# Attention and two gated layers on one core: long fillers on TensorE ahead of the first chunk, another price for the weights' low bits, and a new table of due times

## The chip, the cores and the metric

The kernel runs on one core of a Trainium2 chip. Its engines are TensorE (PE; its weight loads are listed apart as PEld), VectorE (DVE), ScalarE (ACT), GpSimd (POOL) and SyncE (SP), which here only issues DMAs. The metric is the device time of one execution in microseconds. Three runs of the kernel before gave 923.89, 925.21 and 926.55, so the median is 925.21.

## The reference

Attention over q, k, v of shape 4 x 8 x 576 x 64, once over means of four neighbouring rows and once in a band of width 7, then two layers over 2304 tokens of width 512 (weights arrive as 64-bit floats):

```python
out_d = sm_attn(q_d, k_d, v_d)                 # softmax attention over means of 4 rows
out_up = np.repeat(out_d, factor, axis=2)
mask = np.abs(pos[:, None] - pos[None, :]) < factor
scores = scale * np.matmul(q, k.transpose(0, 1, 3, 2))
scores = np.where(mask, scores, -1000000000.0)  # softmax, then @ v: out_local
attn_out = out_up + out_local
x = np.ascontiguousarray(attn_out.transpose(0, 2, 1, 3)).reshape(B * S, H * D)
h = x @ w_in                                   # 512 x 2048
g = np.where(h > 0.0, h, alpha * (np.exp(np.minimum(h, 0.0)) - 1.0))
x = g @ w_out                                  # 2048 x 512
silu = g2 * (1.0 / (1.0 + np.exp(-g2)))        # g2 = x @ w_gate, 512 x 1536
return silu * (x @ w_val) @ w_out2             # 1536 x 512
```

## The kernel before, in words

Nearly every large product is done as three products of two halves (high and low part of each 32-bit operand): `products` issues hi*hi, hi*lo and lo*hi at L1060, L1061 and L1062. The second matrix of the first chunk is the exception, one 32-bit product (L1094).

**Stages.** Tokens of the first layer go in chunks of 288 (three units of 96). The head, ahead of the first chunk, is the attention of the first batch. q and k rows are turned on TensorE (`add_first_batch`, L779) and copied out by ACT and DVE. Four pairs of heads of pooled attention follow (`add_pooled`: scores L857, weights turned L900, values L916). So do six units of local attention (`add_local`: scores L674, mask L692, maxima L697, values L745). Three units make the first chunk's `x`: the sum of both attentions (L1037), its high part (L369 or L371), its low part (L1048). Meanwhile 32 weight tiles arrive, and each is made from its 64-bit words by three operations. These are the low bits (`rest`, L532 on DVE or L534 on ACT), the size (L528 on ACT, into a PSUM bank) and the joining of both (L538 on DVE). An "in" weight is then split: high part L373 on POOL or L369 on ACT, low part L573 on POOL.

**The first chunk** (`add_whole`) takes sixteen rounds. A round is 12 products from `x` into a bank `h`, then an ELU in three steps (ACT L1099, ACT L1100, DVE L1101), then four products L1094 of an earlier round. `h` may lie in two banks only, 6 or 7 (L1081). The ELU's last step gives `h` free.

**What sets the order.** A list scheduler of the kernel's own (`Work`) writes each engine's static order at build time. Every piece of work has a due time and a cost per engine. The table of constants at the top shifts due times, and `start` takes the earliest due piece whose buffers are free. `fetched` lets TensorE's instructions arrive in blocks of 256 words, with `FETCHES` as the time of a block. Where TensorE has nothing ready in the head, `fill` issues a filler product: a short one of 64 columns up to `SHORT` words, a long one of 512 columns later. `warm_up` issues 72 short products at the start. SP issues all loads in one order as well.

**Banks in the head.** Units' scores take banks by this rule, in which `begun` is set when the first product of the first chunk is issued:

```python
def att_bank(late=False):
    return banks.new(lambda: [4, 5] if begun else [6, 0, 1, 2, 3])
```

A bank that holds scores is free when DVE has masked them (L692). The first chunk's sums lie in banks 0 to 3.

## Time and profile before

| | us |
|---|---|
| median of three runs | 925.21 |
| the profiled execution | 921.95 |
| its span, first to last instruction | 920.0 |
| TensorE busy in the span | 905.5 |
| DVE, ACT, POOL busy | 558.6, 520.0, 531.5 |

The profiled execution is 1.95 us longer than its span, and 3.26 us shorter than the median of the runs. TensorE is busy for 98% of the span, so what counts is where it is not busy, and when it does work that is no part of the result (warm-up and fillers). The mean granted clock of TensorE is 0.998 of full speed.

### The profile page before, as it was taken

How to read it: one execution, taken by the hardware profiler on the slowest of the kernel's cores; microseconds unless marked ns; L12 is line 12 of the kernel's file. 1: busy time of each engine (PE TensorE's matmuls, PEld its weight loads, DVE VectorE, ACT ScalarE, POOL GpSimd, SP SyncE). 2: the span in 40 equal slices, each digit the busy share in tenths (PEclk: the TensorE clock that was granted, in tenths of full speed). 3: DMA queues.
4: the chain of work that ended last, by engine and by line, in shares of the span. 5: the costliest groups of instructions: out<-in, count | busy, mean ns of one | idle time of the engine just before them, and what ended most of it. 6: DMA issues, size and time to landing. Idle time of an engine off the chain costs nothing.

```text
span 920.0 us, 20707 instructions
## 1 busy us (share of the span) xinstructions
PE 905.5 (98%) x7937; PEld 818.5 (89%) x7937; DVE 558.6 (61%) x958; ACT 520.0 (57%) x1140; POOL 531.5 (58%) x607
## 2 busy tenths in 40 slices
PE   8799999999999999999999999999999999999998
PEld 6588898989999999999999888888888888999998
DVE  6889877765576349443358475343333258997672
ACT  6888665454556456767555566566545335444441
POOL 6686965655666357698892226989999910000000
PEclk9999999999999999999999999999999999999999
DMA  8999545678645763656497615464624299755231
GB/s 184 325 269 249 102 137 129 131 274 240 119 134 132 222 184 130 226 184 212 167 341 281 238 69 183 160 240 160 240 82 183 81 297 324 260 172 161 92 127 47
DMA packets 193251, 172.17 MB, mean 187 GB/s; under 512 B 96064, under 2 KB 164160, under 8 KB 193152
## 3 DMA queue, kind: packets, MB, share of 16 engines
q1 hardware_dynamic: 193008, 170.58, 59.3%
q8 instruction: 63, 1.03, 0.5%
q14 instruction: 36, 0.29, 0.1%
q10 hardware_dynamic: 144, 0.26, 0.1%
HBM read 111.62 MB, written 59.18 MB: 186 GB/s over the span
## 4 chain that ended last, share of the span: by engine, by line
PE 93%; DMA 3%; DVE 1%; ACT 1%; issue 1%; SPq 1%; ACTq 0%
PE bank L1060 29%; PE bank L1061 28%; PE bank L1062 28%; PE bank L1094 3%; PE bank L674 2%; PE bank L745 2%; DMA w<-in_v_dram 1%; DMA w<-in_k_dram 1%; PE bank L965 1%; PE bank L959 1%; PE bank L1012 1%; PE warm L1753 1%; SPq L770 0%; DVE f L1037 0%; SPq L619 0%
## 5 line engine op out<-in xcount | busy, mean ns | idle before, releaser
L1062 PE MATMUL bank<-xs,wu 128*128 128x512 f32 x336 | 133.2, 396 | 0.0
L1061 PE MATMUL bank<-xs,wu 128*128 128x512 f32 x336 | 133.2, 396 | 0.0
L1060 PE MATMUL bank<-xs,wu 128*128 128x512 f32 x336 | 133.1, 396 | 0.0
L1060 PE MATMUL bank<-os,ys 128*128 128x256 f32 x378 | 107.1, 283 | 0.5 <-DVE o L1273 0.5
L1061 PE MATMUL bank<-os,ys 128*128 128x256 f32 x378 | 107.0, 283 | 0.0
L1062 PE MATMUL bank<-os,ys 128*128 128x256 f32 x378 | 106.9, 283 | 0.0
L1273 DVE TENSOR_TENSOR blk<-bank,blk 128x512 f32<-128x512 f32 x72 | 49.8, 691 | 93.6 <-PE bank L1062 86.6
L1060 PE MATMUL bank<-x,w 128*128 128x288 f32 x320 | 100.3, 314 | 1.9 <-DVE e L1138 1.4
L1060 PE MATMUL bank<-g,w 128*128 128x288 f32 (+1 forms) x320 | 101.0, 316 | 0.0
L1061 PE MATMUL bank<-g,w 128*128 128x288 f32 (+1 forms) x320 | 98.5, 308 | 0.0
L1062 PE MATMUL bank<-g,w 128*128 128x288 f32 (+1 forms) x320 | 98.4, 307 | 0.0
L1062 PE MATMUL bank<-x,w 128*128 128x288 f32 x320 | 94.5, 295 | 0.2 <-issue 0.2
L1061 PE MATMUL bank<-x,w 128*128 128x288 f32 x320 | 94.7, 296 | 0.0
L1270 ACT COPY blk<-bank 128x512 f32<-128x512 f32 x72 | 42.2, 586 | 86.4 <-PE bank L1062 82.5
L1145 POOL TENSOR_TENSOR g<-e,g 128x288 fp32r<-128x288 f32 x64 | 55.4, 867 | 52.2 <-ACT g L369 36.0
L1062 PEld LDWEIGHTS bank<-xs,wu 128*128 128x128 f32 x336 | 63.3, 188 | 15.4
L1061 PEld LDWEIGHTS bank<-xs,wu 128*128 128x128 f32 x336 | 63.3, 188 | 14.2
L1060 PEld LDWEIGHTS bank<-xs,wu 128*128 128x128 f32 x336 | 63.3, 188 | 14.2
L1060 PEld LDWEIGHTS bank<-os,ys 128*128 128x128 f32 x378 | 72.5, 192 | 0.9 <-DVE o L1273 0.7
L1061 PEld LDWEIGHTS bank<-os,ys 128*128 128x128 f32 x378 | 72.5, 192 | 0.2
L1062 PEld LDWEIGHTS bank<-os,ys 128*128 128x128 f32 x378 | 72.5, 192 | 0.0
L1241 POOL TENSOR_TENSOR wu<-s,wu 128x256 fp32r<-128x256 f32 x77 | 60.1, 807 | 12.3 <-ACT wu L1244 12.0
(221 smaller groups left out, 2503.4 us busy)
## 6 DMA issues: line engine op xcount, KB each, us to landing
yr<-yd SPq DMA_DIRECT2D x27, 512.0 KB
yd<-blk SPq DMA_DIRECT2D x24, 512.0 KB
os<-od SPq DMA_DIRECT2D x42, 256.0 KB
w<-in_moe_w_in_dram SPq DMA_DIRECT2D x16, 512.0 KB
w<-in_moe_w_out_dram SPq DMA_DIRECT2D x16, 512.0 KB
wp<-w SPq DMA_DIRECT2D x16, 512.0 KB
wu<-wp SPq DMA_DIRECT2D x16, 512.0 KB
u<-wd SPq DMA_DIRECT2D x32, 256.0 KB
```

The source lines that it names most:

```text
L674: nc.tensor.matmul(sc[j].t[s * QB:(s + 1) * QB, (u * NP + p) * QB:(u * NP + p + 1) * QB], parts["qT"][p].t[j * D:(j + 1) * D, a:a + QB], p ...
L745: nc.tensor.matmul(pvs[r].t[j * D:(j + 1) * D, k * 2 * SB:(k + 1) * 2 * SB], tvs[u].t[rows, (2 * p + j) * D:(2 * p + j + 1) * D], bd.t[row ...
L959: nc.tensor.matmul(sc[0].t[j * D:(j + 1) * D, 2 * G:3 * G], vs0.t[:, w, j], prT0.t[:, j, w], start=(w == 0), stop=(w == 1))
L965: nc.tensor.matmul(sc[j].t[:HALF, u * G:(u + 1) * G], t[:, 0, p, u * HALF:(u + 1) * HALF], t[:, 1, p], start=True, stop=True)
L1060: nc.tensor.matmul(ps, sh, mh, start=first, stop=False, skip_group_check=more)
L1061: nc.tensor.matmul(ps, sh, ml, start=False, stop=False, skip_group_check=more)
L1062: nc.tensor.matmul(ps, sl, mh, start=False, stop=last, skip_group_check=more)
L1094: nc.tensor.matmul(acc[0][i].t[:, :T1], wo.t[:, i * P:(i + 1) * P].bitcast(F32), ge(), start=f == 0, stop=f == NF1 - 1)
L1145: add("pool", 0.86, due - URGENT, lambda e=e, g=g: nc.gpsimd.tensor_tensor(out=g.t[:, 1], in0=e.t, in1=g.t[:, 0], op=ALU.subtract), reads= ...
L1241: return task(engines, n, due, lambda engine=engines[0]: two(engine).tensor_tensor(out=out(), in0=in0(), in1=in1(), op=op), reads, writes, ...
L1270: return add("act", ps_copy, when(m) - 20, lambda: nc.scalar.copy(d(i), ps.t[:, :w]), reads=[ps], writes=of(i))
L1273: return add("dve", ps_sum, when(m) - 20, lambda: nc.vector.tensor_tensor(out=d(i), in0=ps.t[:, :w], in1=d(i), op=ALU.add), reads=[ps], wr ...
```

## The change

Four things change in the code. The warm-up is ten products of 512 columns instead of 72 of 64. `fill` has its long form alone. The planner's price for the low bits on DVE doubles (0.5 to 1.0) and a block of instructions costs it 7.4 instead of 6.0; the price of the pooled weights on ACT rises from 1.28 to 1.66. And nearly all due times of the table move (two of some sixty stand here).

```diff
-    SECOND = 42.48
+    SECOND = 37.84
...
-    AHEAD, BLOCK, FETCHES, RATE = 184, 256, (6.0, 60.0, 3.3), 15.5
+    AHEAD, BLOCK, FETCHES, RATE = 184, 256, (7.4, 60.0, 3.3), 15.5
...
-    URGENT = 24.27
+    URGENT = 21.86
...
-    WARM = 72
-    SHORT = 448.46
+    WARM = 10
...
-            low = add(("act", "dve"), (0.67, 0.5), due - 4, rest, reads=[raw, w.whole], writes=[w], second=3.0)
+            low = add(("act", "dve"), (0.67, 1.0), due - 4, rest, reads=[raw, w.whole], writes=[w], second=3.0)
...
-        add(("act", *EITHER), (1.28, 1.01, 1.14), due + 4.3, weight, reads=[pr, su], writes=[pr], second=1)
+        add(("act", *EITHER), (1.66, 1.01, 1.14), due + 4.3, weight, reads=[pr, su], writes=[pr], second=1)
...
         def warm_up():
             for _ in range(WARM):
-                nc.tensor.matmul(warm[:QB, :64], zeros[:, :QB], zeros[:, :64], start=True, stop=True)
+                nc.tensor.matmul(warm, zeros[:, :P], zeros, start=True, stop=True)
...
-            if work.words < SHORT and (work.border - work.words > 16 or work.arrives < work.now):
-                nc.tensor.matmul(warm[:QB, :64], ident.bitcast(BF16)[:, :QB], ident.bitcast(BF16)[:, :64], start=True, stop=True)
-                return work.FILLS[1]
...
-        add("pe", 1.5 + 0.055 * WARM, -1000.0, warm_up, words=2 * WARM)
+        add("pe", 1.3 + 0.42 * WARM, -1000.0, warm_up, words=2 * WARM)
```

Line numbers of the changed kernel are lower, by one from L478 on and by four from L1753 on (L1060 is L1059 there, L1101 is L1100, L692 is L691).

On TensorE, just ahead of the first chunk, the fourth and later units' scores (`bank<-kT,qT`), fillers (`warm<-ident`) and the first products (`bank<-x,w`) stand so before:

```order
L674 MATMUL bank<-kT,qT 32x32 x64
L1753 LDWEIGHTS ident
L1753 MATMUL warm<-ident 128x512
L1753 LDWEIGHTS ident
L1753 MATMUL warm<-ident 128x512
L1753 LDWEIGHTS ident
L1753 MATMUL warm<-ident 128x512
L1060 MATMUL bank<-x,w 128x288
L1061 MATMUL bank<-x,w 128x288
L1062 MATMUL bank<-x,w 128x288
```

In the changed kernel the same place reads, up to the first products and then around the end of their first group of twelve:

```order
L673 MATMUL bank<-kT,qT 32x32 x32
L1749 LDWEIGHTS ident
L1749 MATMUL warm<-ident 128x512
L1749 LDWEIGHTS ident
L1749 MATMUL warm<-ident 128x512
L673 MATMUL bank<-kT,qT 32x32 x32
L1059 MATMUL bank<-x,w 128x288
```

```order
L1059 MATMUL bank<-x,w 128x288
L1060 MATMUL bank<-x,w 128x288
L1061 MATMUL bank<-x,w 128x288
L673 MATMUL bank<-kT,qT 32x32 x32
L1059 MATMUL bank<-x,w 128x288
L1060 MATMUL bank<-x,w 128x288
L1061 MATMUL bank<-x,w 128x288
```

The last three fillers are gone, and the sixth unit's scores stand behind the first group of products.

On DVE, around the first ELU's last step (`g<-e,bank`), the masks (`w<-bank,mask`), the joining of weights (`w<-bank,w`) and low bits (`w<-w 128x512`) stand so before:

```order
L692 TENSOR_TENSOR w<-bank,mask 128x128 x2
L371 CAST x<-f 128x4x96
L538 SCALAR_TENSOR_TENSOR w<-bank,w 128x512 x2
L697 TENSOR_REDUCE st<-w 128x8
L692 TENSOR_TENSOR w<-bank,mask 128x128 x2
L538 SCALAR_TENSOR_TENSOR w<-bank,w 128x512 x2
L532 TENSOR_SCALAR w<-w 128x512
L538 SCALAR_TENSOR_TENSOR w<-bank,w 128x512 x2
L692 TENSOR_TENSOR w<-bank,mask 128x128 x2
L697 TENSOR_REDUCE st<-w 128x8
L1101 SCALAR_TENSOR_TENSOR g<-e,bank 128x288
```

And now:

```order
L537 SCALAR_TENSOR_TENSOR w<-bank,w 128x512 x2
L531 TENSOR_SCALAR w<-w 128x512
L1100 SCALAR_TENSOR_TENSOR g<-e,bank 128x288
L691 TENSOR_TENSOR w<-bank,mask 128x128 x4
L531 TENSOR_SCALAR w<-w 128x512
L691 TENSOR_TENSOR w<-bank,mask 128x128 x2
L696 TENSOR_REDUCE st<-w 128x8 x2
L699 TENSOR_TENSOR w<-w,st 128x256
L1100 SCALAR_TENSOR_TENSOR g<-e,bank 128x288
```

All three late units are masked ahead of the first ELU before, and behind it now.

On ACT, between the first two rounds' ELUs (`e<-bank`, then `e<-e`), there stand before, with sizes (`bank<-w`), low bits and an exponential of a unit (L703):

```order
L1099 ACTIVATE e<-bank 128x288
L534 ACTIVATE w<-w 128x512
L1100 ACTIVATE e<-e 128x288
L528 ACTIVATE bank<-w 128x512 x2
L703 ACTIVATE w<-w 128x256
L534 ACTIVATE w<-w 128x512
L1099 ACTIVATE e<-bank 128x288
```

And now, with high parts of weights (`CAST w<-w`):

```order
L1098 ACTIVATE e<-bank 128x288
L369 CAST w<-w 128x512
L1099 ACTIVATE e<-e 128x288
L369 CAST w<-w 128x512 x4
L1098 ACTIVATE e<-bank 128x288
L533 ACTIVATE w<-w 128x512
```

Five casts now stand on ACT between the two first steps where four weight operations and one exponential stood.

## Rows read from the trace of the kernel before

**Rows 1.** Stages: us, busy by engine (instructions), granted clock, DMA share, GB/s.

```profile
core 0: us, PE busy (x) PEld busy (x) DVE busy (x) ACT busy (x) POOL busy (x), PEclk, DMA share, GB/s
0.00:45.05 45.05, 37.62 (x819) 26.77 (x820) 33.55 (x88) 32.44 (x99) 30.18 (x50) 0.98 0.92 254
45.05:50.90 5.85, 5.23 (x32) 4.70 (x30) 4.17 (x11) 3.99 (x9) 4.54 (x6) 0.85 1.08 309
50.90:300.00 249.10, 246.60 (x3376) 224.94 (x3377) 186.70 (x379) 150.59 (x359) 169.87 (x201) 1.00 0.66 172
300.00:913.60 613.60, 613.59 (x3697) 559.86 (x3695) 333.74 (x483) 332.63 (x674) 326.87 (x353) 1.00 0.55 189
```

**Rows 2.** TensorE's waits: us in total, times, longest.

```profile
PE bank L674 <- issue: 4.9, 2, 3.9
PE bank L1060 <- DVE e L1138: 1.4, 2, 1.2
PE bank L1060 <- DVE g L1101: 0.4, 1, 0.4
PE bank L1062 <- issue: 0.2, 1, 0.2
```

**Rows 3.** Stages between TensorE's gaps in the head.

```profile
16.02:21.70 5.68, 4.73 (x129) 2.60 (x127) 4.56 (x14) 3.48 (x15) 5.44 (x8) 1.00 0.72 133
21.70:28.45 6.75, 6.17 (x127) 3.92 (x127) 5.20 (x20) 6.60 (x28) 6.07 (x8) 1.00 0.88 244
28.45:36.55 8.10, 7.73 (x120) 4.92 (x121) 7.43 (x21) 7.31 (x22) 3.48 (x6) 1.00 1.06 377
36.55:43.00 6.45, 2.57 (x128) 1.74 (x128) 5.26 (x10) 5.46 (x11) 6.40 (x7) 1.00 1.09 331
43.00:50.80 7.80, 7.18 (x127) 6.04 (x126) 5.54 (x13) 4.24 (x9) 4.75 (x6) 0.78 1.09 292
```

**Rows 4.** DMA queues in the first 60 us: packets, MB, share of 16 engines.

```profile
q8 instruction: 6, 0.10, 0.8%
```

**Rows 5.** The chain of waits, 4 to 47 us: start, us, what.

```profile
4.62 8.19 DMA w<-in_k_dram
...
39.18 3.90 issue
43.08 1.14 PE bank L674 x66
44.22 1.40 PE warm L1753 x3
45.62 0.24 PE bank L1060
```

**Rows 6.** Stages after the longest gap, for the clock.

```profile
46.00:46.60 0.60, 0.60 (x4) 0.60 (x3) 0.60 (x2) 0.00 (x0) 0.60 (x1) 0.50 1.09 312
47.00:48.00 1.00, 1.00 (x9) 1.00 (x9) 0.54 (x3) 0.19 (x1) 0.92 (x2) 1.00 1.06 319
```

**Rows 7.** TensorE's timeline: start, us, what, count, idle before.

```profile
1.19 4.02 PE L1744 MATMUL warm<-bd 128*32 128x64 bf16 x72 [1.19 <-DVE bd L1739]
7.82 0.67 PE L1750 MATMUL warm<-ident 128*32 128x64 bf16 x17
17.25 2.33 PE L1753 MATMUL warm<-ident 128*128 128x512 bf16 x10
23.74 0.76 PE L674 MATMUL bank<-kT,qT 64*32 64x32 f32 x64
47.35 0.29 PE L1061 MATMUL bank<-x,w 128*128 128x288 f32 x1
47.48 0.29 PE L1062 MATMUL bank<-x,w 128*128 128x288 f32 x1
```

**Rows 8.** ACT, DVE and POOL's timelines, 33 to 50 us.

```profile
33.93 1.47 ACT L369 COPY bd<-w 32x192 f32<-32x192 f32 x4
41.38 1.00 POOL L1048 TENSOR_TENSOR x<-f,x 128x384 fp32r<-128x384 f32 x1
44.73 0.61 POOL L373 CAST w<-w 128x512 fp32r<-128x512 f32 x1 [1.78 <-DVE w L538]
47.81 0.41 ACT L1099 ACTIVATE e<-bank 128x288 f32<-128x288 f32 x1 [1.86 <-PE bank L1062]
49.16 0.46 DVE L1101 SCALAR_TENSOR_TENSOR g<-e,bank 128x288 f32<-128x288 f32 x1 [1.62 <-ACT e L1100]
```

**Rows 9.** Groups of low bits up to 110 us: busy, mean ns, idle before.

```profile
L532 DVE TENSOR_SCALAR w<-w 128x512 uint32<-128x512 uint32 x16 | 13.6, 869 | 0.8 <-DMA w<-in_moe_w_in_dram 0.8
L534 ACT ACTIVATE w<-w 128x512 int32<-128x512 uint32 x16 | 10.7, 672 | 0.4 <-DMA w<-in_moe_w_in_dram 0.4
```

More of the change, by code (lines that the diff above doesn't have):

```diff
@@ L396, in bank @@
         return banks.new(lambda: places)
-    STEP2 = 7.4
-    START = 46.02
-    STEP0 = 4.64
-    STEP = 4.67
+    STEP2 = 7.48
+    START = 45.73
+    STEP0 = 4.76
+    STEP = 4.78
     FIRST = -40.0
-    VALUES = -97.38
-    LATER = 72.97
-    POOLED = -2.71
-    EARLY = -0.67
-    PREFER = -36.56
-    EAGER = 23.32
-    URGENT = 24.27
-    FREE = 0.67
+    VALUES = -97.16
+    LATER = 66.08
+    POOLED = -1.9
+    EARLY = 0.53
+    PREFER = -41.28
+    EAGER = 24.97
+    URGENT = 21.86
+    FREE = 3.78
     SLACK = 0.0
-    LOAD = 12.31
+    LOAD = 12.03
     KEEP0 = 2.24
-    KEEP1 = 2.13
+    KEEP1 = -0.06
     DIRECT = 2, 3, 1
-    PARTS1 = 107.75
-    UNIT1 = 2.72
+    PARTS1 = 102.3
+    UNIT1 = 14.77
     LAGG = 2
-    MASK = 18.05
+    MASK = 16.99
     TAILW = True
-    WOS0 = -2.01
-    WOS1 = -0.35
-    EARLYA = 30.39
-    EARLYB = 12.08
-    LOADA = 70.96
-    LOADB = 7.36
-    O2A = 5.25
-    O2B = 35.36
-    ELU1 = 36.59
-    ELU0 = 21.64
-    UNIT2 = 24.15
-    UNIT0 = 18.13
-    RAW = 32.57
-    DEPTH = 6
-    PARTS = 17.2
-    OUT = -8.62
-    SUMS = 5.66
-    SUMS3 = 32.26
-    SECOND2 = 17.38
-    LATE = 83.1
-    AWAY0 = 1.2
-    AWAY1 = 5.97
-    LO1 = 14.36
-    HI1 = 8.8
-    LO2 = 23.59
-    HI2 = 22.77
-    LO3 = 27.06
-    HI3 = -37.65
-    KEYS = 70.97
-    POOL1 = -0.63
-    POOL0 = 21.7
-    POOL2 = 16.09
-    LOCAL = -6.11
-    ROWS = 28.01
-    INPUT = -2.63
+    WOS0 = -8.19
+    WOS1 = 1.03
+    EARLYA = 26.28
+    EARLYB = 21.63
+    LOADA = 68.1
+    LOADB = 11.79
+    O2A = 10.44
+    O2B = 35.98
+    ELU1 = 37.65
+    ELU0 = 25.38
+    UNIT2 = 30.41
+    UNIT0 = 24.33
+    RAW = 32.93
+    DEPTH = 6
+    PARTS = 16.02
+    OUT = -8.56
+    SUMS = 7.14
+    SUMS3 = 36.87
+    SECOND2 = 14.96
+    LATE = 85.86
+    AWAY0 = 1.16
+    AWAY1 = 5.85
+    LO1 = 14.17
+    HI1 = 8.38
+    LO2 = 21.69
+    HI2 = 27.22
+    LO3 = 22.21
+    HI3 = -53.35
+    KEYS = 71.74
+    POOL1 = -5.69
+    POOL0 = 22.41
+    POOL2 = 14.82
+    LOCAL = -5.79
+    ROWS = 25.37
+    INPUT = -6.54
     order = [(c, f) for c in range(NC) for f in range(NF1)]
```

## The prediction

> **What bounds the kernel now.** I read the stages first. From 300 to 913.6 us TensorE is busy for 613.59 of 613.60 us, and from 50.9 to 300 for 246.6 of 249.1 [rows 1]. The work there is the same after the change, so at most 2.5 us can be won behind the head, and a new wait there can only cost. The head is the first 45.05 us, up to the first product of the first chunk. There TensorE is idle for 7.4 us, and much of its busy time is warm-up and fillers.
>
> The waits come next. The longest, 4.9 us in two pieces, 3.9 the longest, stands at the scores L674 and is put down to "issue": nothing that the profile shows was waited for [rows 2]. I read it as TensorE's instructions not being there yet, for three reasons. I counted matrix and weight-load instructions between the ends of gaps. The five stages have 256, 254, 241, 256 and 253 [rows 3]; waits on semaphores are instructions too, and fill most of what lacks to 256. In the first 60 us a queue for instructions moves six packets and 0.10 MB [rows 4], so about 16 KB each, which for 256 instructions is 64 bytes an instruction. And the stages, taken from gap end to gap end, last 5.7, 6.75, 8.1, 6.45 and 7.8 us, whatever work is in them. So from 16 us on each block comes 6 to 8 us after TensorE stepped into the one before it, and the head is a chain of such fetches: 16.0, 21.7, 28.45, 36.55, 43.0. In the second and third the other work is nearly as late as the block, since TensorE is busy for 6.17 of 6.75 and 7.73 of 8.10 us.
>
> The Trainium skill (Runtime: NRT & Kernel Launch, Instruction fetch mechanics) says that instructions come in blocks of 256, the next while one runs, and that crossing a boundary is mostly hidden. The trace agrees on the 256 and not on the rest: 4.9 us of waits stand at the boundaries [rows 2]. By "hidden" the number of fillers would not matter at all; the sum below comes to nearly the same by another road.
>
> The chain of waits shows what follows the last fetch: 3.90 us of idle, 1.14 of scores, 1.40 of three fillers, then the first products [rows 5]. The clock fell in that gap. At 46.0 to 46.6 it is granted at 0.50, the 1.2 GHz level, and it is back at 1.00 by 47 [rows 6]. The price is read from the products: 0.24 us each at the lower level [rows 5], 0.13 from start to start at the higher [rows 7].
>
> **The change part by part.**
>
> *Warm-up.* 72 short products took 4.02 us [rows 7]. Ten long ones have no row at that place. Ten fillers of the same shape took 2.33 us at the higher level [rows 7], and three took 1.40 at the lower [rows 5], so 2.3 to 4.7 us; I take 4.5. The first turned rows move by -1.7 to +0.7 us. I cost that at nothing: the last k rows land at 12.8 us [rows 5], and all scores need them. Uncovered it would cost up to 0.7.
>
> *Fillers in the first 16 us.* 17 short ones took 0.67 us [rows 7]; three long ones at 0.23 stand in their place and take 0.7. No time, but fewer instructions.
>
> *The chain of fetches.* Ahead of the first scores there stood 440 instructions besides waits (144 warm-up, 162 short and 6 long fillers, the rest real); now there are 184, since 124 and 162 go and 30 come with long fillers. The difference is 256, one whole block. So the boundaries fall on the same places of what follows: the middle of the second unit's scores, the turning of pooled weights, the third unit's values, the fifth unit's scores. One fetch is saved, but an early one that nobody waited for. The four that make the chain start from the same place at the same time and should take as long. I take 0 and keep -2 to +2: the five stages spread by 2.4 us. The work beside it does not run ahead either: the spread of the third unit's weights on ACT, which its values need, ended at 35.4 [rows 8], and by the order ACT has one set of pooled weights less ahead of it but two copies more, and DVE one set more.
>
> *The last stretch.* From 43.08 on, the rest of the fifth unit's scores is left, about 16 of 64 records (0.2 us), and then the first group of twelve products comes at once. The three fillers are gone: -1.40. The clock is then low for twelve products instead of six, so 6 x (0.24 - 0.13): +0.66. The sixth unit's scores (0.76 us [rows 7]) move behind the group and are done either way: 0.
>
> *A new wait.* The masks of the last three units stand behind the first ELU on DVE now. Until they run, the fifth unit's scores hold bank 6, one of the two that `h` may use. So the second group of products must take bank 7 again, which the first ELU's last step frees. Before, the group's last product started at 47.48 [rows 7] and was through at about 47.6; the first step started at 47.81 and the last ended at 49.62 [rows 8], 2.0 us after the group. ACT has one operation between the ELU's steps then (0.67 us [rows 9]) and one now (a cast, 0.61 by POOL's [rows 8]). The first group now ends at 43.3 + 12 x 0.24 = 46.2; the ELU is done at 48.3. TensorE has 0.76 us of scores to do meanwhile and waits from 47.0 to 48.5: +1.5. Behind it on TensorE stands everything. The bounds: 0, should the ELU run in the order's best case beside the low clock's end, and 2.5, should DVE, which by the order has seven low-bits operations (0.87 each [rows 9]) and eight joinings to do between the third unit's values and it, come to it 1 us late.
>
> *Waits that go.* The wait for the ELU (0.4) and the one at the next boundary (0.2) [rows 2] go, since four products L1094 are put ahead of the third group and give the block time: -0.6.
>
> *Low bits.* Counted in the order, ACT does 17 of 32 now and 16 before. One operation of 0.67 us on ACT for one of 0.87 on DVE [rows 9] is 0; the edit hardly does what its words say.
>
> *Loads and the rest.* On SP the late units' value rows now stand ahead of the last eight pairs of weights. These are used 20 us or more later, and SP has nothing else queued that TensorE waits for: 0. Behind 50.9 us 2.5 us of waits stand, 1.4 of them for one ELU (L1138) [rows 1, 2]. Another order has others. I take 0, bounds -2 and +3.
>
> The sum is -1.40 + 0.66 + 1.5 - 0.6 = +0.2 us, on 921.95 of the profiled execution, so 922.1. The median of the runs is 3.26 above that execution. I put the change on the median: 925.4.
>
> **The rivals.**
>
> *The stall goes.* If the fetch behind the third unit's values comes 2 us sooner, the gap is short, the clock stays up, and the first group starts when its low part is ready, at 42.4 (L1048, 41.38 + 1.00 [rows 8]). That is 2.7 us earlier than 45.05, 0.6 less for the clock and 0.6 for the waits, and the new wait stays at about 0.9: -3.0, or 922.2. For it speaks that the stages spread between 5.7 and 8.1 us; against it that other work was nearly as late in two of them. Waits behind the head that go (up to 2.5) lead to the same side.
>
> *ACT holds the second round up.* Five casts stand on ACT where the second round's first step waits. POOL's cast waited 1.78 us for the joining on DVE once [rows 8]. If ACT's casts wait so twice, ACT, strictly in order, brings the second ELU 3 us late. The fourth group needs that bank and stands still, with all behind it. It decides from the point where DVE's eighth joining comes later than 48 us. Price: 3.0 to 4.0, so 928.4 to 929.4.
>
> *The change does not do what it says.* The low bits stay where they were, and the long warm-up saves a fetch that nobody waited for. This is part of the forecast itself; without the new wait it would be -1.4, so 923.8, still no change that can be measured.
>
> **How the numbers follow.** About 0.3%, 2.8 us, is what a measurement of this kernel can tell from no change. Forecast: 0.47, with its own range 922.6 to 928. The stall or later waits go: 0.30, around 922, part of it over 922.4. ACT, or another new wait behind the head, holds TensorE: 0.23, around 928.8. Faster by over 0.3% has then 0.28, the same 0.49, slower 0.23. The range for 8 in 10 goes from 920.8, where fetches and later waits both give 2 us, to 929.2.
>
> **What would show it.** Right: a gap of about 4 us in the fifth unit's scores, ending near 43; the first product within 0.5 us of its end, at 0.24 us each; a wait of 1 to 2 us ahead of the second group, released by DVE's L1100; TensorE full from 300 us on. Wrong: the gap under 2 us or at another place, a first product before 42.5, no wait at the second group, or more than 4 us idle between 51 and 300.

## The result and the profile after

The changed kernel took 930.52 us (median of 4 runs, 929.0 to 930.87) against 925.10 (4 runs, 923.89 to 926.55): a ratio of 1.0055, interval 1.0037 to 1.0073. That is 5.4 us slower, where I had forecast 925.4, no change. A later set of runs gave 1.0070 (1.0051 to 1.0089). The profiled execution took 930.87 us with a span of 929.1, so it lies at its median; that of before lay 3.2 us under its own. The 9.1 us between the two spans are therefore more than the change is worth.

The stages of the changed kernel, in the columns of [rows 1]: up to the first product, the first rounds, the rest of the first chunks, and the long stretch.

```profile
0.00:45.92 45.92, 39.33 (x615) 24.15 (x615) 31.90 (x80) 30.55 (x95) 27.47 (x46) 0.85 0.95 252
45.92:56.60 10.68, 7.83 (x111) 6.82 (x96) 8.51 (x21) 8.89 (x19) 9.98 (x10) 0.84 1.06 293
56.60:300.00 243.40, 238.34 (x3328) 218.21 (x3327) 186.60 (x367) 146.68 (x348) 158.28 (x193) 0.99 0.64 164
300.00:922.20 622.20, 620.37 (x3744) 566.14 (x3743) 332.11 (x485) 338.90 (x688) 325.22 (x358) 1.00 0.55 189
```

TensorE idles 2.9 us in the first rounds and 6.9 us behind them (243.40 - 238.34 and 622.20 - 620.37), where before had 0.6 and 2.5 [rows 1]. Its waits behind 100 us, in the changed kernel:

```profile
PE bank L1011 <- DVE sm L691: 2.5, 2, 1.4
PE bank L1059 <- DVE e L1137: 1.7, 2, 1.0
PE bank L673 <- issue: 1.6, 1, 1.6
PE bank L958 <- DVE prT L371: 0.6, 1, 0.6
```

Before had 1.4 of L1060 (now L1059) on DVE e [rows 2], and its trace has none of the others behind 100 us. A second execution of the same program, called again below, shows which of these belong to the order:

```profile
PE bank L1011 <- DVE sm L691: 2.6, 2, 1.4
PE bank L673 <- issue: 2.2, 1, 2.2
PE bank L1059 <- DVE e L1137: 1.7, 2, 1.0
PE bank L958 <- DVE prT L371: 0.6, 1, 0.6
```

Three of the four rows come back to a tenth. In the head the first execution has its two waits at the second round. TensorE's timeline (start, us, what, idle before it):

```profile
45.67 0.32 PE L673 MATMUL bank<-kT,qT 64*32 64x32 f32 x22 [1.96 <-issue]
45.92 0.40 PE L1059 MATMUL bank<-x,w 128*128 128x288 f32 x1
...
50.51 0.76 PE L673 MATMUL bank<-kT,qT 64*32 64x32 f32 x64 [2.43 <-DVE w L537]
51.68 0.38 PE L1059 MATMUL bank<-x,w 128*128 128x288 f32 x1 [0.41 <-DVE g L1100]
```

And the granted clock stood at 0.50 for long parts of the head, where before has 1.00 up to 43 us:

```profile
24.60:28.00 3.40, 3.40 (x76) 2.00 (x74) 2.73 (x13) 1.81 (x9) 2.87 (x5) 0.50 1.01 266
28.00:31.40 3.40, 3.31 (x34) 2.51 (x33) 3.01 (x8) 3.36 (x12) 2.32 (x3) 1.00 1.05 382
31.40:41.60 10.20, 10.20 (x132) 6.38 (x130) 5.63 (x17) 6.70 (x20) 2.59 (x3) 0.50 1.06 370
```

So three suspects: the clock in the head, the waits at the second round, and the waits behind 180 us.

### The profile page after: what moved, and what is told of

It is laid out like the page before. It is cut to its first block, busy times and chain, and to the rows that moved or that the text cites. A ratio compares the mean times of both kernels' runs of the same rounds, so it can differ in the third digit from the quotient of the medians.

```text
span 929.1 us, 20387 instructions
## 1 busy us (share of the span) xinstructions
PE 908.3 (98%) x7797; PEld 817.5 (88%) x7797; DVE 559.6 (60%) x952; ACT 525.4 (57%) x1148; POOL 521.0 (56%) x604
## 4 chain that ended last, share of the span: by engine, by line
PE 89%; DMA 4%; DVE 3%; SPq 1%; POOL 1%; issue 1%; ACT 1%; DVEq 0%; ACTq 0%
PE bank L1059 28%; PE bank L1060 27%; PE bank L1061 27%; PE bank L1093 3%; DMA w<-in_v_dram 2%; PE bank L744 1%; PE bank L673 1%; DMA w<-in_k_dram 1%; PE bank L964 1%; PE bank L958 1%; DMA w<-in_moe_w_in_dram 1%; PE bank L1011 1%; DVE f L1036 0%; DVE t L1240 0%; DVE mid L512 0%
## 5 line engine op out<-in xcount | busy, mean ns | idle before, releaser
L1060 PE MATMUL bank<-xs,wu 128*128 128x512 f32 x336 | 133.2, 396 | 0.0
L1059 PE MATMUL bank<-xs,wu 128*128 128x512 f32 x336 | 133.1, 396 | 0.0
L1059 PE MATMUL bank<-os,ys 128*128 128x256 f32 x378 | 107.1, 283 | 0.5 <-DVE o L1272 0.5
L1060 PE MATMUL bank<-os,ys 128*128 128x256 f32 x378 | 107.0, 283 | 0.0
L1059 PE MATMUL bank<-x,w 128*128 128x288 f32 x320 | 100.5, 314 | 2.1 <-DVE e L1137 1.7
L1059 PE MATMUL bank<-g,w 128*128 128x288 f32 (+1 forms) x320 | 101.2, 316 | 0.0
L1272 DVE TENSOR_TENSOR blk<-bank,blk 128x512 f32<-128x512 f32 x72 | 49.7, 691 | 82.2 <-PE bank L1061 74.2
L1060 PE MATMUL bank<-g,w 128*128 128x288 f32 (+1 forms) x320 | 98.8, 309 | 0.0
L1060 PE MATMUL bank<-x,w 128*128 128x288 f32 x320 | 95.0, 297 | 0.0
L1059 PEld LDWEIGHTS bank<-xs,wu 128*128 128x128 f32 x336 | 63.3, 188 | 14.1
L1060 PEld LDWEIGHTS bank<-xs,wu 128*128 128x128 f32 x336 | 63.3, 188 | 14.1
L1059 PEld LDWEIGHTS bank<-os,ys 128*128 128x128 f32 x378 | 72.5, 192 | 0.9 <-DVE o L1272 0.7
L1060 PEld LDWEIGHTS bank<-os,ys 128*128 128x128 f32 x378 | 72.5, 192 | 0.2
L1240 POOL TENSOR_TENSOR wu<-s,wu 128x256 fp32r<-128x256 f32 x78 | 57.2, 762 | 16.5 <-ACT wu L1243 16.1
```

The lines of the kernel that those rows point to most:

```text
L1059: nc.tensor.matmul(ps, sh, mh, start=first, stop=False, skip_group_check=more)
L1060: nc.tensor.matmul(ps, sh, ml, start=False, stop=False, skip_group_check=more)
L1240: return task(engines, n, due, lambda engine=engines[0]: two(engine).tensor_tensor(out=out(), in0=in0(), in1=in1(), op=op), reads, writes, ...
L1272: return add("dve", ps_sum, when(m) - 20, lambda: nc.vector.tensor_tensor(out=d(i), in0=ps.t[:, :w], in1=d(i), op=ALU.add), reads=[ps], wr ...
```

## The experiments

Ratios are to runs of the kernel before on the same chip, with their intervals.

**Parts of the change, with a new order each time.** e_fill has the long warm-up and fillers alone, e_price the planner's three numbers alone, e_notable all but the table.

The first of them, then the second:

```diff
-    WARM = 72
-    SHORT = 448.46
+    WARM = 10
-                nc.tensor.matmul(warm[:QB, :64], zeros[:, :QB], zeros[:, :64], start=True, stop=True)
+                nc.tensor.matmul(warm, zeros[:, :P], zeros, start=True, stop=True)
-            if work.words < SHORT and (work.border - work.words > 16 or work.arrives < work.now):
...
```

```diff
-    AHEAD, BLOCK, FETCHES, RATE = 184, 256, (6.0, 60.0, 3.3), 15.5
+    AHEAD, BLOCK, FETCHES, RATE = 184, 256, (7.4, 60.0, 3.3), 15.5
-            low = add(("act", "dve"), (0.67, 0.5), due - 4, rest, ...
+            low = add(("act", "dve"), (0.67, 1.0), due - 4, rest, ...
-        add(("act", *EITHER), (1.28, 1.01, 1.14), due + 4.3, weight, ...
+        add(("act", *EITHER), (1.66, 1.01, 1.14), due + 4.3, weight, ...
```

> The kernel before with the ten long warm-up products and only long fillers; table, fetch numbers and prices as before, so the order moves little beyond what the fewer fillers bring. Theory A (TensorE's clock falls to 0.50 in the head, as the trace after shows at 24.6-28.0, 31.4-41.7 and 51.9-55.3 us, because of the fillers and of the place of the block boundaries): stretches of 0.50 ahead of 42 us here too, third unit's values 2 to 4 us later than 36, first product at 45.5 to 47, total 2 to 5 us over before. Rival B (the new order of the last units' scores and masks costs it, 2.8 us of waits between 46 and 52 and 4 to 6 us by 400 us): this kernel keeps all masks ahead of the first ELU, so within 1.5 us of before, whatever the clock does ahead of 40 us.

> The kernel before with the three changed numbers of the planner alone (7.4 for 6.0 us, the two prices); warm-up, short fillers and table as before. Its order has 24 products of the first round ahead of the sixth unit's scores and four masks behind the first ELU. Theory A (clock and fillers cost it): clock 1.00 up to about 43 us as before, first product at 45 +- 1, total within 2 us of before. Rival B (order of scores and masks costs it): a wait of 1 to 3 us between the first product and 52 us, behind an ELU or a size, and 2 to 5 us over before.

> The whole change but for the table of numbers, which is that of before. In the head its order is nearly that of the changed kernel: masks of the last units behind the first ELU, the sixth unit's scores behind the first twelve products. Theory A (clock) and theory B (order in the head) both expect the head of the changed kernel: clock 0.50 in parts of 24 to 42 us, first product at 46, a wait of 2 to 3 us near 48, and 3 to 5 us over before. Theory C (the table costs it, by the waits of 4.4 us that stand between 183 and 370 us): those waits are gone and the total is within 2 us of before, or at least 3 us under the changed kernel.

Measured: 1.0160 (1.0141 to 1.0180), 1.0045 (1.0028 to 1.0062), 1.0084 (1.0064 to 1.0104). No theory had 15 us for e_fill. e_price came out 4 us over, as theory B had, but without B's wait: between 45 and 64 us its TensorE waits once, 0.75 us, for `x`. Each edit makes the planner write another order for all engines, so these runs don't show what an edit does by itself; they show that three other orders are also slower, and that the table by itself is not what costs: without it, it is slower still (C falls).

**The same edit with the order kept.** v_before_long is the kernel before, every engine in its old order, with ten long warm-up products for the 72 and fifteen long fillers for the 81 short ones. f_before_short and v_before_nofill go the other way: behind 17 us each filler is a short product, or none.

In the order of these names:

```diff
-            for _ in range(WARM):
-                nc.tensor.matmul(warm[:QB, :64], zeros[:, :QB], zeros[:, :64], start=True, stop=True)
+            for _ in range(10):
+                nc.tensor.matmul(warm, zeros[:, :P], zeros, start=True, stop=True)
...
+                shorts.append(1)
+                if len(shorts) * 15 // 81 == (len(shorts) - 1) * 15 // 81:
+                    return work.FILLS[1]
```

```diff
+            if work.now > 17.0:
+                nc.tensor.matmul(warm[:QB, :64], ident.bitcast(BF16)[:, :QB], ident.bitcast(BF16)[:, :64], start=True, stop=True)
+                return work.FILLS[0]
```

```diff
+            if work.now > 17.0:
+                return work.FILLS[0]
```

> The kernel before with its order kept on every engine, but with ten long warm-up products for the 72 short ones and fifteen long fillers for the 81 short ones, so 256 or 257 fewer instructions ahead of the first scores: the part of the change on TensorE without the new order. My prediction's step (the edit itself costs nothing, since the blocks begin at the same places of the work): first product at 45 +- 0.7, a gap of 3 to 4 us in the fifth unit's scores, total within 1.5 us of before. Rival T (long fillers themselves make TensorE late): first product 1.5 us or more later and 2 to 5 us over before.

> The kernel before, every engine in the same order, but each filler later than 17 us is a short product of 32x64 instead of a long one, so TensorE has less to do between 17 and 43 us. Theory A (a lighter TensorE lets its clock fall in the head, and that costs time): stretches granted at 0.50 ahead of 42 us, where before has none; the third unit's values later than 36.1 by 1 to 3 us or the gap at 39.2 moved, first product at 45.5 to 47, total +1.5 to +4 us. Rival F (the head is set by instruction blocks and other engines alone): the fillers' time was idle time anyway, first product at 45 +- 0.5, total within 1.5 us of before in spite of the low clock.

> The kernel before without any filler later than 17 us, order kept: 66 instructions less on TensorE between 17 and 43 us. With short fillers in their place the clock was granted at 0.50 from 23 to 50 us and the total was the same, so the fillers' warmth is not needed. Theory F: the block that ended in the fifth unit's scores ends 66 instructions later in the work, behind them, so the first products no longer wait for it; first product at 42.5 to 44.5, at the lower clock for some 3 us, total 0.5 to 2.5 us under before. Rival: DVE and ACT set the first and the second round, as in the changed kernel, and the total is within 1 us of before; or the blocks end at bad places further on, as with twenty more warm-up products, and it is 2 to 5 us over.

Measured: 1.0010 (1.0000 to 1.0021), 0.9991 (0.9982 to 0.9999) and 1.0010 (0.9997 to 1.0023). The edit by itself costs about 1 us, 2 at most; by the total rival T falls. The heads did not follow the forecasts: the first products came at 47.1, 46.2 and 46.9 us, later than my step and theory F had them, and v_before_long had no gap in the fifth unit's scores at all. TensorE, at 0.50 from 30.7 to 40.9 us, reached that boundary of blocks at 44.0, went on without a wait, and waited 1.0 us for a mask later. And the clock in the head costs nothing in the total: the stages of f_before_short stand at 0.50 throughout,

```profile
24.60:28.00 3.40, 3.35 (x86) 2.47 (x83) 2.45 (x10) 2.29 (x10) 2.80 (x4) 0.50 1.04 242
31.40:41.60 10.20, 9.88 (x236) 8.06 (x237) 7.56 (x20) 7.62 (x22) 4.54 (x6) 0.50 1.06 377
46.00:51.00 5.00, 5.00 (x24) 4.91 (x24) 3.50 (x9) 2.81 (x6) 4.36 (x5) 0.54 1.09 325
```

and it is as fast as before, though its first product came 1.1 us later than in before's profile. Theory A falls for the head of the old order.

**The head of the changed kernel.** e_mask puts the last units' masks first on DVE, and the planner then puts all scores ahead of the products. v_after_move4 moves four warm-up products to 21.9 us and nothing else. v_after_light (its control: v_before_light) does the sizes and joinings of fourteen pairs on half of their columns and leaves the other half out.

In this order:

```diff
-        add("dve", cost(0.56, 0.28), due + 3 - FREE, masked, reads=sc, writes=[sm], after=masks)
+        add("dve", cost(0.56, 0.28), due + 3 - FREE - (120.0 if UPC <= i < NU and n == 1 else 0.0), masked, reads=sc, writes=[sm], after=masks)
```

```diff
+            [work.filler() for _ in range(4 if (b, p) == (0, 3) else 0)]
-            for _ in range(WARM):
+            for _ in range(WARM - 4):
```

```diff
-            due = dues[n]
+            due, part = dues[n], 256 if n < 14 else 512
-                nc.scalar.activation(ps.t, raw.t[:, :, 1].bitcast(F32), AF.Prelu, scale=2.0 ** -BIAS, alpha=MINUS)
+                nc.scalar.activation(ps.t[:, :part], raw.t[:, :part, 1].bitcast(F32), AF.Prelu, scale=2.0 ** -BIAS, alpha=MINUS)
-                t, p = w.t.bitcast(I32), ps.t.bitcast(I32)
+                t, p = w.t.bitcast(I32)[:, :part], ps.t.bitcast(I32)[:, :part]
```

> The changed kernel with the masks of the last three units put first on DVE; the planner then puts all 64 score products ahead of the first products, and 36 products run before the first L1093. Theory A (clock in the head): clock stretches at 0.50 from 24 to 42 us as in the changed kernel, first product at 46 or later, so total 2 to 4 us over before although the wait near 48 us is gone. Theory B (order of scores and masks): the 2.8 us between 46 and 52 go, total within 2 us of before, 925 to 927. Theory C (waits behind the head): the idle time of 4.4 us between 183 and 370 us stays unless the order there moves with it.

> The changed kernel with four of its ten warm-up products moved to just ahead of the fourth pooled unit's scores, where TensorE stands idle for 0.7 + 0.2 us at 21.9 to 23.2; nothing else moves. Theory A (the idle time at 20.9 to 23.2 lets the clock fall to 0.50 at 24.6, and that makes the head late): no stretch at 0.50 at 24.6 to 28, fillers and turnings there at full speed, third unit's values at 37 to 39 instead of 40.5, total 1.5 to 4 us under the changed kernel. Rival F (blocks and other engines set the head): first product at 46 +- 0.5, total within 1 us of the changed kernel. If the clock falls all the same, the row of idle time is not what brings it.

> The changed kernel, order kept on every engine, with the sizes (ACT) and the joinings (DVE) of the first fourteen pairs of weights done on 256 of 512 columns; half of the low bits of these pairs are left out. Between 42.2 and 50 us nine sizes and eight joinings stand on ACT and DVE; with the durations of the trace (0.63 and 0.68 at 512 columns; half the columns estimated at 0.38 and 0.36) each saves 0.25 and 0.32 us, 2 to 2.5 us on either engine. Theory O (the weights' pairs come late in the new order, and DVE and ACT hold the sixth unit's scores and the second round): the waits of 2.43 and 0.41 us at 48 to 52 shrink to 0 to 1 us, the second round starts 1.5 to 2.5 us earlier, total 1.5 to 3 us under the changed kernel. Rival (bank order or TensorE itself): waits stay within 0.5 us, total within 1 us.

> The same halving in the kernel before, as a control. There eight sizes and five joinings are done by 42.2 us, and DVE has 1.8 and 1.6 us of idle time between 42 and 49. Theory O: nothing there waits for them, total within 1 us of before. Rival (the vector engines bound the head in any order): 1.5 to 3 us under before.

> The changed kernel once more beside these, for more runs: 930.5 +- 1.5. All theories agree on its time. Its profile tells what a second execution shares with the first: the waits on DVE (2.4 + 0.4 at 48 to 52; L1011 1.1 and 1.4; L1059 0.7 and 1.0) within 0.3 us each and the wait at the block's end near 202, if they come from the order and the blocks; the stretches at 0.50 at other places, if these are chance.

Measured: e_mask 1.0030 (1.0016 to 1.0043), v_after_move4 1.0068 (1.0046 to 1.0090), v_after_light 1.0074 (1.0053 to 1.0095), v_before_light 0.9994 (0.9983 to 1.0005), after_again 1.0070 (1.0051 to 1.0089). v_after_move4 had no stretch at 0.50 at 24.6 to 28 and gained nothing, but it had one at 34.3 to 41.2 instead, so it tells little of theory A. v_after_light, against 1.0070, gained nothing either: theory O, that late sizes and joinings cost the time, falls by the total, as far as the intervals go. Its one wait at the second round is 1.11 us ahead of the second group, as 0.93 in after_again, and that is the first ELU's chain, which begins when the first group is done. The wait of 2.43 us for banks 4 and 5 comes and goes: of the eight executions of the changed order four have it (2.43, 0.99, 1.23 and, in v_after_move4, 2.21), and four, v_after_light among them, have none.

```profile
50.63 0.76 PE L673 MATMUL bank<-kT,qT 64*32 64x32 f32 x64 [2.21 <-DVE w L537]
```

e_mask is 2 to 4 us better than the changed kernel, but it moved waits behind 180 us as well (L1011's fell to 0.2), so it doesn't tell the head from the rest; theory A, too, had its total (2 to 4 us over before).

**The place of the blocks.** Forty instructions more ahead of everything (twenty short products), or the 72 short warm-up products in the changed kernel (124 more), with the order kept; and the latter on top of e_mask.

In v_before_warm20, v_after_warm20, and v_after_warm72 and v_mask_warm72:

```diff
-            for _ in range(WARM):
+            for _ in range(WARM + 20):
```

```diff
+            [nc.tensor.matmul(warm[:QB, :64], zeros[:, :QB], zeros[:, :64], start=True, stop=True) for _ in range(20)]
```

```diff
-            for _ in range(WARM):
-                nc.tensor.matmul(warm, zeros[:, :P], zeros, start=True, stop=True)
+            for _ in range(72):
+                nc.tensor.matmul(warm[:QB, :64], zeros[:, :QB], zeros[:, :64], start=True, stop=True)
```

> The kernel before with twenty more short warm-up products, so that each block of 256 instructions begins 40 instructions earlier in the work; nothing else moves. Theory F (the blocks set the head): the wait of 3.9 us in the fifth unit's scores ends 2 to 3 us earlier or goes, first product at 42 to 44 instead of 45.05, total 1.5 to 3 us under before. Theory A (TensorE's clock decides): total follows the stretches at 0.50, and only if none more come does the gain stay. Rival N (the place of the blocks doesn't matter): within 1 us.

> The changed kernel with twenty short products ahead of its warm-up, 40 instructions, so that all later blocks begin 40 instructions earlier in the work; nothing else moves. Theory F (place of the blocks): the waits at block ends, 0.63 at 20.9, 1.96 at 43.7 and 1.61 at 201.8 us, stand 40 instructions earlier in the work or go; first product at 43.5 to 45.5. The wait of 2.43 at 48 us for the sixth unit's scores stays, 2 to 3 us, since it hangs on DVE and two banks. Total 0 to 3 us under the changed kernel. Theory A: as far as stretches at 0.50 at 24 to 42 us stay, the total does too, within 1 us.

> The changed kernel with the 72 short warm-up products of before for its ten long ones; nothing else moves, and each block begins 124 instructions earlier in the work, half a block. Theory F (place of the blocks): the wait of 1.6 us at 201.8, which stood at a block's end in the changed kernel and with small moves of the head, goes, with the stretch at 0.50 that follows it in some runs: 1.5 to 3 us, if no other block's end finds such a place. Theory O (order: the waits for masks and banks, 2.84 us at 48 to 52 and 3.6 us of L1011, L958 and L1059 behind 186 us): these stay within 0.5 us each. So total 927 to 930 if both hold; 930 to 932 if the block's place doesn't matter.

> Masks first and 72 short warm-up products together: the order of the run with masks first (927.7), with each block 124 instructions earlier. If the two causes add up, the wait of 2.35 us at the block's end near 201 goes, and the total is 927.7 - 2.4 = 925.3, or 923.6 if the stretch at 0.50 behind it goes too: level with before. If other block ends find bad places, 927 to 930.

Measured: 1.0054 (1.0039 to 1.0070), 1.0076 (1.0058 to 1.0094), 1.0050 (1.0030 to 1.0070), 1.0074 (1.0053 to 1.0095). Theory F was right that a block's end can cost a few us and wrong that moving it helps: the wait at 201 went in v_after_warm72, and one of 1.62 came at 218.5. v_before_warm20 got 2.06 at 148.6 and 1.15 at 215.1, and its first product did not come earlier (45.1); it was 5 us slower than before, and these two waits are 3.2 of its profile. Counted in TensorE's instructions (weight loads and waits on semaphores included), the waits of over 0.15 us put down to "issue" behind 60 us stand whole multiples of 256 apart, to within one, in all fourteen executions of the two orders. Added up they were 1.4 to 2.4 us in eight executions of the changed order and 0.2 to 4.3 in six of the old one; the mean is 2.0 in both. So this is a lottery that the profiled execution of before had won (0.2); it does not tell the two orders apart.

**The waits behind 180 us.** But for the block's end at 202 us, they come from DVE. Its timeline in the changed kernel, then GpSimd's (POOL), then TensorE's wait:

```profile
182.83 0.44 DVE L1137 SCALAR_TENSOR_TENSOR e<-e,bank 128x288 f32<-128x288 f32 x1
183.19 3.98 DVE L512 SCALAR_TENSOR_TENSOR mid<-mid,w 128x256 int32<-128x256 int32 x1
187.09 0.74 DVE L691 TENSOR_TENSOR sm<-bank,mask 128x256 f32<-128x256 f32 x2
```

```profile
183.05 1.14 POOL L997 TENSOR_TENSOR pr<-pr,su 72x576 f32<-72x576 f32 x1 [0.38 <-DVE su L994]
184.16 0.79 POOL L1144 TENSOR_TENSOR g<-e,g 128x288 fp32r<-128x288 f32 x1
184.91 1.97 POOL L1047 TENSOR_TENSOR x<-f,x 128x384 fp32r<-128x384 f32 x2
186.84 0.90 POOL L941 TENSOR_TENSOR praw<-praw 72x256 f32<-72x256 f32 x1
```

```profile
187.65 0.68 PE L1011 MATMUL bank<-ident,pr 72*72 72x72 f32 x8 [1.06 <-DVE sm L691]
```

The joining L512 takes 0.44 us as a rule (the median of 24) and 3.98 here. It begins 0.14 us after a row of four GpSimd operations began, and ends 0.3 us after the fourth did; the masks stand behind it, and L1011 waits for the bank that they free. The same at 260 us: two adds L1036 (0.71 by their median) take 4.22 and end 0.4 us after GpSimd's row does, at 264.03.

```profile
260.23 4.22 DVE L1036 TENSOR_TENSOR f<-f,xdT 128x384 f32<-128x384 f32 x2
264.37 0.41 DVE L1378 TENSOR_TENSOR mid<-w 128x256 f32<-128x256 f32 x1
264.71 0.74 DVE L691 TENSOR_TENSOR sm<-bank,mask 128x256 f32<-128x256 f32 x2
```

```profile
261.17 0.65 POOL L942 TENSOR_TENSOR vs<-praw 72x128 f32<-72x128 f32 x1
261.79 0.72 POOL L1378 TENSOR_TENSOR mid<-w 128x256 f32<-128x256 f32 x1
262.47 1.56 POOL L1144 TENSOR_TENSOR g<-e,g 128x288 fp32r<-128x288 f32 x2
```

The Trainium skill (SBUF — State Buffer, Who interferes with whom) says that an operation of DVE with two inputs in SBUF and one of GpSimd that reads SBUF can't run at once, and the later waits. The trace agrees: L512 and L1036 have two such inputs, while L1137 and L691, with one of theirs in a bank, ran at their usual length beside GpSimd. All nineteen traces bear it out. L512 on 256 columns began 189 times with no GpSimd operation under way (memsets aside) and never took over 0.43 us; it began 265 times beside one and took 0.80 by the median, up to 3.99. L691, 194 times beside one, never took over 0.43. Operations with one input are held too: the low bits (L531 here) took 0.42 by the median without GpSimd and 0.84, up to 2.98, beside it, and the casts to `x` 0.36 and 0.76. Transposes were not: L811 took 0.77 by the median without GpSimd, and, 291 times beside it, never over 0.79.

The length by itself costs nothing. The longest such operation in the kernel before, the first of two L1458, took 11.2 us beside a row of L1241 on GpSimd, while TensorE, by [rows 1], lost nothing there:

```profile
465.32 12.75 DVE L1458 SCALAR_TENSOR_TENSOR y<-e,y 128x864 f32<-128x864 f32 x2 [5.76 <-ACT e L1457]
```

What costs is such a wait ahead of something that TensorE needs.

v_after_skip leaves out these three operations of DVE, v_after_quarter does them on a quarter of the columns; the order is kept.

```diff
-            nc.vector.scalar_tensor_tensor(
+            nth["words"] == 6 or nc.vector.scalar_tensor_tensor(
-            two(engine).tensor_tensor(
+            (engine, nth[engine]) in skip or two(engine).tensor_tensor(
```

```diff
+            nth["words"] += 1; w = 64 if nth["words"] == 6 else 256; t = u.t.bitcast(I32)[:, :w]
+            nth[engine] += 1; w = 1 if (engine, nth[engine]) in (("dve", 9), ("dve", 10)) else NP
```

> The changed kernel, order kept, with three operations of DVE left out: the joining L512 of one pair of weights at 183 us and the two adds L1036 at 260 us, which stand right ahead of masks L691 for which TensorE's L1011 waits in every execution (1.06 to 1.24 at 186, 1.36 to 1.47 at 264; then 0.64 of L958). In the trace they took 3.98 us instead of 0.41 and 4.22 instead of 1.9, and ended when a row of GpSimd operations ended. Theory P (DVE, held by GpSimd's rows, makes the masks late, by the new order): both L1011 waits fall to 0 to 0.3 us, L958's may stay; total 2 to 3.5 us under the changed kernel, 927.2 to 928.8. Rival D (DVE is late there anyway): other DVE work brings the masks as late, waits within 0.4 us of before, total within 1 us of the changed kernel.

> The same three operations of DVE, now on a quarter of their columns (64 of 256, 96 of 384; the rest of these tiles is left as it was). Theory P (they wait for the end of GpSimd's row, and their own length is nothing): L512 still takes 3.5 to 4 us and ends at the end of GpSimd's second L1047, the second L1036 still ends within 0.5 us of the end of GpSimd's last L1144, both L1011 waits stay at 0.7 to 1.4 us, total within 1.2 us of the changed kernel. Rival L (they are long in themselves, from their own data): 3.98 becomes 1 us, 4.22 about 1, the waits go, total as with the three left out.

Measured: v_after_skip 1.0012 (1.0003 to 1.0022), v_after_quarter 1.0048 (1.0033 to 1.0063). Without three operations, 1.9 us of DVE work by their medians (0.44 + 2 x 0.71), most of the loss is gone: 1.0070 to 1.0012 is 5.4 us (2.7 to 8 by the ends of the two intervals), more than theory P had. Rival D falls. TensorE's waits behind 100 us there:

```profile
PE bank L1059 <- DVE e L1137: 1.7, 2, 1.0
PE bank L673 <- issue: 1.6, 1, 1.6
PE bank L958 <- DVE prT L371: 0.3, 1, 0.3
```

Both L1011 rows are gone. What each place cost can be read off the traces, since both kernels issue the same products in the same order, and each product can be set beside its twin. Against v_after_skip the six executions of the changed order with these three operations in full (after, after_again, v_after_move4, v_after_warm20, v_after_warm72, v_after_light) lose 1.2 to 1.6 us at the first place (182 to 189 us of v_after_skip) and 1.6 to 3.3 at the second (257 to 273), together 3.0 to 4.8. The second is 1.6 to 1.7 where the clock stays up behind it, and 3.2 to 3.3 in the four executions where it fell to 0.50 there, between 266 and 274 us.

How much of the rest is clock is not shown. In five of the six it also fell to 0.50 behind the wait at a block's end near 202 or 219 us (204.5 to 207.9 in the second execution); a stretch like that one loses at most half its 3.4 us against full speed. In the profiles of v_after_skip and v_after_quarter it did not fall behind the head, nor in any of six executions of the old order, before the last few us. But in e_mask, which has no L1011 wait on DVE, it fell at 204.6 to 208.0 all the same, so that stretch needs no such wait. And the profiled execution of v_after_skip is the fastest of its twelve, with a mean clock of 0.996 where the others have 0.990 to 0.994; that of v_after_quarter is the fastest of its six. The stage 190 to 300 us of the second execution, of v_after_skip and of e_mask:

```profile
190.00:300.00 110.00, 105.69 (x1683) 99.40 (x1683) 76.95 (x155) 58.38 (x145) 61.27 (x78) 0.98 0.65 178
```

```profile
190.00:300.00 110.00, 108.06 (x1713) 102.14 (x1713) 75.05 (x151) 60.68 (x149) 62.96 (x80) 1.00 0.69 190
```

```profile
190.00:300.00 110.00, 106.04 (x1686) 99.59 (x1687) 73.28 (x154) 60.30 (x151) 61.36 (x80) 0.98 0.68 187
```

v_after_quarter settles what the 3.98 us were. DVE, then GpSimd:

```profile
179.84 3.78 DVE L512 SCALAR_TENSOR_TENSOR mid<-mid,w 128x64 int32<-128x64 int32 x1
183.54 0.74 DVE L691 TENSOR_TENSOR sm<-bank,mask 128x256 f32<-128x256 f32 x2
```

```profile
179.71 1.14 POOL L997 TENSOR_TENSOR pr<-pr,su 72x576 f32<-72x576 f32 x1 [0.38 <-DVE su L994]
180.82 0.79 POOL L1144 TENSOR_TENSOR g<-e,g 128x288 fp32r<-128x288 f32 x1
181.57 1.97 POOL L1047 TENSOR_TENSOR x<-f,x 128x384 fp32r<-128x384 f32 x2
183.50 0.72 POOL L941 TENSOR_TENSOR praw<-praw 72x256 f32<-72x256 f32 x1
```

A quarter of the work, and as long: it is waiting. Rival L falls there. It ends at 183.62, just behind the fourth operation of GpSimd's row. The fifth, L941, had then begun; why it was let in there and not earlier, no run shows, and none moved GpSimd's row away instead. At the second place theory P was half wrong: the two small adds found room ahead of the row (1.14 us together), and the next operation, L1378, was held for 2.88 in their place; L1011 then waited 0.8 instead of 1.4. The total came out 2.0 us under the changed kernel (1.0048 against 1.0070), where theory P allowed 1.2. No run of the seventeen beats the kernel before by what can be told from no change.

## Why the prediction was wrong

*Warm-up, early fillers and the edit on TensorE, 0:* held in the total. With the order kept they cost 1.0010 (1.0000 to 1.0021). It did not hold in its steps: v_before_long had no gap in the fifth unit's scores, and its first product came at 47.1.

*The chain of fetches, 0 (-2 to +2):* the places of the blocks held (waits in the second and the fifth unit's scores), their times did not. I had 36.55 and 43.0 for the last two; in the first execution TensorE stepped into them at 40.8 and 45.7, and in after_again the last gap, of 3.75 us, ended at 46.0. The first product came at 45.9 and 46.3, not at 43.3. TensorE ran at half speed over fillers and turnings there. It cost less than it looks: six executions of the old order, before's own among them, have the 61st product of `x` and a weight -0.3 to +2.4 us from that of before's profile, 1.2 on average, and eight executions of the changed order 0.7 to 4.3, 2.6 on average. So the head lost about 1.4 us, by means of executions that spread by more, where I had +0.2.

*The last stretch, -1.40 + 0.66:* right in kind. The products follow the scores at once; they ran at 0.13 in the first execution and at 0.24 in the second.

*The new wait, 1.5 (0 to 2.5):* right in place, and in size (1.0 to 1.2) in the four executions where the sixth unit's scores found their banks free. In the other four that wait comes on top, for banks 4 and 5, which I had not seen: together 2.84 in the first execution, 2.74, 2.73 and 1.81, three of them over the bound.

*Waits that go, -0.6:* held. No execution of the changed order waits for the ELU at the third group or at the next boundary.

*Waits behind the head, 0 (-2 to +3):* this is the step that failed. I wrote that another order has other waits and took nothing. Here it has 4.4 to 4.9 us of waits on DVE in each of six executions, where before has 1.4 (a wait of 0.5 for L1272 that both have is left out), and stretches at 0.50 besides. My own sign for it, over 4 us idle between 51 and 300, came up: 5.06 from 56.6 on. Two places account for most of it: product by product they cost 3.0 to 4.8 us, the clock behind the second included, and taking three operations of DVE away at 183 and 260 us gave back 5.4 of 6.5 (1.0070 against 1.0012). Its mechanism stood in the trace of before. There an add L1037 took 2.94 us beside GpSimd's three, and TensorE's longest wait behind the head, 1.2 of [rows 2], followed it; DVE, GpSimd and TensorE in turn:

```profile
155.66 2.94 DVE L1037 TENSOR_TENSOR f<-f,xdT 128x384 f32<-128x384 f32 x1
```

```profile
155.66 2.53 POOL L1037 TENSOR_TENSOR f<-f,xdT 128x384 f32<-128x384 f32 x3
```

```profile
160.03 0.40 PE L1060 MATMUL bank<-x,w 128*128 128x288 f32 x1 [1.19 <-DVE e L1138]
```

I read that row as "a wait for one ELU" and did not ask why the ELU was late. With it I could have looked in the new order for DVE operations on two SBUF tiles beside long rows of GpSimd's, and the price of one (1.2) times the number of places would have been a term above 0.

*The base:* the profiled execution of before stood 3.2 us under its median, and by its waits at block ends (0.2, where the mean is 2.0) it was a fortunate one. Taking its stages as the normal ones, I believed that behind 50.9 us only 2.5 us were to be had.

*The rivals:* "another new wait holds TensorE", 928.8 with 0.23, was nearest in time, but its price was worked out for ACT in the second round, and there TensorE waited for DVE alone. Left open: why the clock fell at different places in two executions and what it cost behind the head, what gives or spares a wait at a block's end, and which of the changed numbers brought the two bad places.

## What to carry to other kernels

When a change makes a planner write a new order, price the order, not the edit: run the edit with the order kept, and the order by itself. An operation several times as long as its like is a wait in disguise; look at what the neighbouring engine did from its start to its end, and let no operation of a form that was held here (two inputs in SBUF above all, but low bits and casts too) stand on DVE ahead of something that TensorE needs, while GpSimd works off a row. And a kernel that is full to the last us has a trace of luck in it: compare medians before stages.

## What the runs showed of the hardware

An operation on 64 columns took 3.78 us beside four GpSimd operations back to back: it began 0.13 us behind the first and ended 0.08 us behind the fourth. Another, in the kernel before, took 11.2 us beside a longer row. TensorE at 0.50 from 23 to 51 us cost nothing in a head that waits for other things (f_before_short, 0.9991). The same TensorE instructions waited 0.2 us at block ends behind 60 us in one execution of the kernel before, and 1.9 in v_before_light.
